# Decode kernel, last stage: output projection by heads from 1 KB rows, head sums normalised straight into the tile of the queries, batches 0 to 6 at low priority

## The chip, the cores and the metric

One core of one Trainium2 chip. The metric is the device time of one execution in microseconds (us). Each result below is a median of several executions, and a ratio to the kernel before from executions on the same chip in alternation. The profile is one execution. Executions of one and the same kernel spread by some 6 us here (1141.9 to 1148.5 for the kernel before in one series), so a microsecond is read from a trace, stage by stage, and the total only confirms it.

In the profiles PE is TensorE and PEld its weight loads, DVE is VectorE, ACT ScalarE, POOL GpSimd, and SP SyncE, which issues the transfers. A pair is one weight load and its matmul. "[2.52 <-issue]" means 2.52 us of idle time in which the engine waited for nothing that the profile shows; I call that a stop. The granted clock is given as a share of full speed.

## The reference, cut to what matters

```python
B, Sq, D = 8, 1, 512;  Hq, Hkv, Sk, Dh = 32, 8, 8192, 128;  F = 1792     # bf16
x = x + A(layernorm(x))      # q = x@wq; softmax(q k^T / sqrt(Dh)) v over the caches; @ wo
x = x + B(layernorm(x))      # silu(x@w1) @ w2
x = x + A(layernorm(x))      # the same caches and weights once more
x = x + B(layernorm(x))
```

The two caches are 268 MB. K and V of a (batch, group) pair are 2 MB each. The kernel keeps the turned keys of one batch on the chip and reuses them for the second layer, but V is read once in each layer. A group is one cache head with its four query heads.

## The kernel before: the parts concerned

Every piece of work is a node with an engine, an assumed duration, a priority (a lower number goes first) and its dependences. A planner runs the nodes on a model clock and emits them in that order.

The sums of one unit (batch, group) are evacuated, gathered over partitions on PE, and multiplied with wo. The kernel multiplies a row of the sums with the row of wo that lies on the same partition. It loads wo so that a partition holds four neighbouring rows, 4 KB in one run, and brings the sums into that arrangement by four matmuls ("spread") and a masked product ("own"):

```python
wo_v = A_wo.rearrange("(g p j) d -> p g (j d)", g=G, j=R)          # 4 KB runs
...
hn = plan.add(f"hi{u}", "ACT", 0.42, high, pr - 2, [vs[-1]])       # L1034, after the last V quarter
ln = plan.add(f"lo{u}", "DVE", 0.45, low, pr - 2, [hn, ...])       # L1038
es.append(plan.add(f"g{u}", "PE", 0.2, gather, pr - 2, [ln, ...])) # L1046
if not h["own_rows"]:        # batches 0 to 6, second layer: normalise into qab
    h["n"] = plan.add(f"n{u}", "DVE", 0.17, norm, pr - 2, [es[-1], h["rc"]])
else:                        # first layer, and batch 7: copy, spread, own
    n = plan.add(f"cast{u}", "ACT", 0.2, cast, pr - 2, [es[-1]])
    n = plan.add(f"spread{u}", "PE", 0.2, spread, pr - 2, [n])     # L1068
    h["n"] = plan.add(f"own{u}", "DVE", 0.17, own, pr - 2, [n, h["rc"], ...])
```

The last stage: the V units of batch 7 (groups 2 to 7) go into the slots of the keys as these are scored, the last one in parts of half, quarter, quarter. wo is read whole (2 x 2 MB) just ahead of them. Batches 0 to 6 go through the second layer's projection and FFN together ("d"), batch 7 alone at the end ("e").

```python
load_wo_all()
w = free_yt[0]
done = [h["n"] for h in ends] + [made[1]["n"], second_q[G - 1]]
for g in range(G):
    w = out_proj_b("d", g, fin, w, done)         # prio = count[0] - G: ahead of all V units
w = x2_node("d", 0, fin, count[0] - G, [w])
fed = ffn_nodes("d", count[0] - G, 0, fin, [w, second_q[G - 1]])
for g, h in enumerate(made):
    if g > 1:
        values(h, at=g)                          # V from a key slot
    ...
    w = out_proj_a(h, w, h["u"])
n = x2_node("e", fin, 1, big, [w])
n = ffn_nodes("e", big, fin, 1, [n, fed])
```

## Time and profile before

| | before |
|---|---|
| time, median of 4 executions | 1144.05 us (1143.73 to 1146.1) |
| span of the profiled execution | 1141.4 us |
| DMA queue busy, share of the span | 98.2% |
| PE / DVE busy | 63% / 53% |
| last V byte lands | 1122.6 us |
| last V quarter starts on PE | 1128.4 us |

Only the last stage changes, so the page's shares of the whole span say little. The two last rows are what matters: the stream ends at 1122.6 us and the work behind it takes 18.8 us more. The prediction below shows the lines for both.

### The profile page before, as it was taken

The numbers are of one execution on the slowest core, as the hardware profiler recorded it, in microseconds if no ns is written. First come the engines' busy times: TensorE is split into PE (matmuls) and PEld (weight loads), VectorE is DVE, ScalarE is ACT, GpSimd is POOL, SyncE is SP. The second block draws the span as 40 slices with busy tenths as digits, with TensorE's granted clock in tenths as the row PEclk, the third lists the DMA queues.
The fourth block names the chain that finished last, engine by engine and source line by source line (L and its number), as shares of the span: only waits on it lengthen the run. The fifth ranks groups of instructions, "written<-read, shape, count | busy, mean of one in ns | idle before, by whom it ended". The sixth has DMA issues, their size and how long they took to land.

```text
span 1141.4 us, 32325 instructions
## 1 busy us (share of the span) xinstructions
PE 717.8 (63%) x13900; PEld 397.8 (35%) x13900; DVE 609.9 (53%) x1768; ACT 155.1 (14%) x517; POOL 117.4 (10%) x295
## 2 busy tenths in 40 slices
PE   2545566676665765656665766567656576565886
PEld 1322333343332433324332433334333243333554
DVE  5753566626664356634666355752656535663341
ACT  0010111111111111111111121111211111111111
POOL 1000011000110001100111000100111000110110
PEclk9665686657776666766666575755767666775675
DMA  9999999999999999999999999999999999999992
GB/s 370 420 418 399 375 412 422 412 390 413 422 421 402 409 418 420 419 393 395 414 421 420 382 419 417 423 400 389 420 424 418 405 409 419 421 422 398 387 424 113
DMA packets 75855, 458.78 MB, mean 402 GB/s; under 512 B 8112, under 2 KB 9920, under 8 KB 48064
## 3 DMA queue, kind: packets, MB, share of 16 engines
q1 hardware_dynamic: 75712, 456.70, 98.2%
q8 instruction: 110, 1.80, 0.6%
q14 instruction: 33, 0.27, 0.1%
HBM read 456.66 MB, written 0.01 MB: 400 GB/s over the span
## 4 chain that ended last, share of the span: by engine, by line
DMA 66%; PE 20%; DVE 6%; issue 5%; ACT 1%; SPq 1%; POOL 1%; POOLq 0%; DVEq 0%; ACTq 0%
DMA ring<-in_A_v_cache_dram 49%; DMA ring<-in_A_wo_dram 8%; PE sc L898 8%; PE ot L1024 7%; DMA kts<-in_A_k_cache_dram 4%; DVE kts L843 3%; DMA kts<-in_A_v_cache_dram 2%; DMA w<-in_B_w_dram 2%; PE misc L725 1%; DMA ring<-in_A_wq_dram 1%; SPq L414 1%; PE ex L1046 1%; PE yt L1098 1%; PE sc L930 1%; DVE part L1038 1%
## 5 line engine op out<-in xcount | busy, mean ns | idle before, releaser
L1024 PE MATMUL ot<-ring,p 128*8 128x256 bf16 x3904 | 240.0, 371 | 185.3 <-DMA ring<-in_A_v_cache_dram 176.3
L843 DVE STREAM_TRANSPOSE kts<-kts 128x1024 uint32<-128x1024 uint32 x256 | 308.1, 1223 | 28.1 <-DMA kts<-in_A_k_cache_dram 27.9
L898 PE MATMUL sc<-kts,bd 128*32 128x256 bf16 x4096 | 284.2, 407 | 33.7 <-DVE kts L843 18.7
L1024 PEld LDWEIGHTS ot<-ring,p 128*8 128x8 bf16 x3904 | 86.0, 96 | 259.9 <-DMA ring<-in_A_v_cache_dram 220.2
L898 PEld LDWEIGHTS sc<-kts,bd 128*32 128x32 bf16 x4096 | 117.5, 117 | 106.3 <-DVE bd L881 26.6
L924 ACT ACTIVATE p<-sc,small 128x256 bf16<-128x256 f32 x128 | 60.8, 475 | 410.0 <-DVE small L919 266.5
L915 POOL PARTITION_ALL_REDUCE small<-small x128 | 47.8, 373 | 616.8 <-DVE small L911 529.0
L1038 DVE TENSOR_TENSOR part<-ot,p 128x256 bf16<-128x256 f32 x128 | 53.1, 415 | 97.6 <-ACT p L1034 56.6
L1034 ACT ACTIVATE p<-ot 128x256 bf16<-128x256 f32 x128 | 49.1, 384 | 410.0 <-PE ot L1024 402.2
L930 PE MATMUL sc<-p,ident 128*32 128x256 bf16 x512 | 42.8, 322 | 82.4 <-ACT p L924 81.4
L881 DVE TENSOR_TENSOR bd<-sc,mask 128x64 bf16<-128x64 f32 x128 | 27.7, 216 | 104.3 <-PE sc L898 98.9
L944 POOL PARTITION_ALL_REDUCE small<-small x128 | 55.4, 433 | 227.5 <-DVE small L940 227.5
L910 DVE TENSOR_REDUCE small<-sc 128x1 f32<-128x256 f32 x128 | 53.3, 416 | 34.6 <-PE sc L898 34.6
L937 DVE STREAM_TRANSPOSE p<-sc 128x256 bf16<-128x256 bf16 x128 | 56.7, 443 | 9.3 <-PE sc L930 6.8
L930 PEld LDWEIGHTS sc<-p,ident 128*32 128x32 bf16 x512 | 15.2, 108 | 110.7 <-ACT p L924 109.0
L1098 PE MATMUL yt<-z,ring 128*128 128x4 bf16 x1024 | 36.8, 166 | 20.5 <-DMA ring<-in_A_wo_dram 19.9
L1046 PE MATMUL ex<-diag,p 128*128 128x4 bf16 x256 | 25.9, 171 | 33.8 <-DVE part L1038 19.0
L1098 PEld LDWEIGHTS yt<-z,ring 128*128 128x128 bf16 x1024 | 31.4, 102 | 43.1 <-DMA ring<-in_A_wo_dram 30.2
L1046 PEld LDWEIGHTS ex<-diag,p 128*128 128x128 bf16 x256 | 16.5, 104 | 77.6 <-ACT p L1034 44.5
L940 DVE TENSOR_SCALAR small<-hm,small 128x4 f32<-128x4 f32 x128 | 27.0, 211 | 29.6 <-ACT p L924 29.2
L1075 DVE TENSOR_TENSOR z<-ex,rc 128x16 bf16<-128x16 f32 x72 | 12.0, 166 | 55.1 <-PE ex L1068 54.8
L919 DVE SCALAR_TENSOR_TENSOR small<-small,hm 128x4 f32<-128x4 f32 x128 | 19.3, 151 | 39.7 <-POOL small L915 39.7
(102 smaller groups left out, 549.7 us busy)
## 6 DMA issues: line engine op xcount, KB each, us to landing
ring<-in_A_v_cache_dram SPq DMA_DIRECT2D x146, 1024.0 KB, 12.5
kts<-in_A_k_cache_dram SPq DMA_DIRECT2D x64, 2048.0 KB, 12.1
ring<-in_A_v_cache_dram SPq DMA_DIRECT2D x196, 512.0 KB, 7.7
ring<-in_A_wo_dram SPq DMA_DIRECT2D x64, 512.0 KB, 12.0
ring<-in_A_wq_dram SPq DMA_DIRECT2D x20, 512.0 KB, 12.4
kts<-in_A_v_cache_dram SPq DMA_DIRECT2D x5, 2048.0 KB, 23.9
kts<-in_A_wo_dram SPq DMA_DIRECT2D x2, 2048.0 KB, 14.2
w<-in_B_w_dram SPq DMA_DIRECT2D x2, 1792.0 KB, 14.9
```

The lines of the kernel that those rows point to most:

```text
L843: op(dve, lambda: dve.transpose(v, v), reads=[], writes=[res("kt", g)], add=(q > 0))
L898: steps.append(lambda t=t, y=y, w=w: pe.matmul(sc[32 * t:32 * t + 32, 0:256], w, kv[:, 2 * t + y, q], start=(q == 0 and y == 0), stop=(q = ...
L910: op(dve, lambda: dve.tensor_reduce(mxr[si], sv, AX.X, ALU.max), reads=[res(*scr)], writes=[res("mxr", si)])
L924: op(act, lambda: act.activation(pt[:, :], sv, ACT.Exp, bias=bias[si], scale=SM_SCALE, accum_out=rsum[si]), reads=[res(*scr), res("bias", ...
L930: steps = [lambda P=P: pe.matmul(sc[32 * P:32 * P + 32, 256:512], src[:, P], pt[:, :], start=True, stop=True) for P in range(4)]
L937: op(dve, lambda: dve.transpose(pt[:, :], src), reads=[res(*scr)], writes=[res("p", sm)])
L944: op(pool, lambda: pool.partition_all_reduce(ssa[si], ssm[si], 128, bass.bass_isa.ReduceOp.add), reads=[res("mxp", si)], writes=[res("mxa" ...
L1024: steps.append(lambda t=t, c=c, k=k: pe.matmul(ot[32 * t:32 * t + 2 * R, 0:2 * DH], pt[:, k:k + 2 * R], vt[:, c, t], start=(P == 0 and c = ...
L1034: op(act, lambda: act.activation(pt[:, :], ot[:, 0:2 * DH], ACT.Copy), reads=[res("ot", o)], writes=[res("p", sm)])
L1038: op(dve, lambda: dve.tensor_tensor(part[:, :], ot[:, 0:2 * DH], pt[:, :], ALU.subtract), reads=[res("ot", o), res("p", sm)], writes=[res( ...
L1046: steps.append(lambda k=k, src=src, y=y: pe.matmul(EX[:, 0:R], src[:, y * DH:y * DH + DH], diag[:, R * y:R * y + R], start=(k == 0 and y = ...
L1098: steps.append(lambda j=j, dt=dt: pe.matmul(YT[:, dt * R:(dt + 1) * R], w[:, j, dt * 128:(dt + 1) * 128], zt[:, R * j:R * j + R], start=(g ...
```

## The change

The intent is less PE work in the last stage and a punctual PE. wo is read so that a partition holds one row of each head (1 KB runs). Then the normalised sums are multiplied with it as they are: no copy, spread or mask. The first residual needs no sum over j. Batches 0 to 6 come last in the choice of what PE does next.

```diff
-        own_rows = layer == 0 or b == NB - 1
+        own_rows = layer == 0
...
-    def out_proj_b(tag, g, nb, prev, deps):     # spread (PE), own (DVE), mul (PE) per group
-        prio = count[0] - G
-        ...
+    def out_proj_b(tag, g, b0, nb, prio, deps): # mul only, straight from qab
+            w = slot(WO_AT[g // 4]).rearrange("p (h d) -> p h d", h=16)
+                        YT[:, dt * nb:(dt + 1) * nb], w[:, R * (g % 4) + r, dt * 128:(dt + 1) * 128],
+                        qab[:, b0:b0 + nb, R * g + r], ...
...
+    def x2_of(tag, b0, nb, prio, deps):         # one add in place of reduce and add
...
-                dma(sp, slot(k).rearrange("p (g n) -> p g n", g=4), wo_v[:, 4 * i:4 * i + 4, :], ksem[k],
+                dma(sp, slot(k).rearrange("p (h d) -> p h d", h=16),
+                    A_wo.rearrange("(h p) d -> p h d", p=128)[:, 16 * i:16 * i + 16, :], ksem[k],
...
+    mid = count[0] + 20
     for g in range(G):
-        w = out_proj_b("d", g, fin, w, done)
+        w = out_proj_b("d", g, 0, fin, mid, [w] + done)
-    w = x2_node("d", 0, fin, count[0] - G, [w])
-    fed = ffn_nodes("d", count[0] - G, 0, fin, [w, second_q[G - 1]])
+    w = x2_of("d", 0, fin, mid, [w])
+    fed = ffn_nodes("d", mid, 0, fin, [w, second_q[G - 1]])
     for g, h in enumerate(made):
         if g > 1:
             values(h, at=g)
-        ...
-        w = out_proj_a(h, w, h["u"])
+        w = out_proj_b("e", g, fin, 1, h["u"], [h["n"], w])
```

Two assumed durations of the planner (variance and root for seven batches) were raised as well; they only place nodes.

More of the change, by code (lines that the diff above doesn't have):

```diff
@@ L490, in _build @@
     big_hs = tail[:, 512:512 + FT * NB]
-    big_y = tail[:, 768:768 + 2 * NB * KT].bitcast(FP32)
     def norm_nodes(tag, prio, b0, nb, deps):
@@ L558, in norm_nodes @@
         a = plan.add(f"{tag}.squares", "PE", 0.05 + 0.2 * nb, squares, prio, [a, x])
-        v = plan.add(f"{tag}.var", "DVE", 0.3, vari, prio, [a])
-        r = plan.add(f"{tag}.root", "POOL", 0.65, root, prio, [v])
+        v = plan.add(f"{tag}.var", "DVE", 0.3 if nb == 1 else 0.6, vari, prio, [a])
+        r = plan.add(f"{tag}.root", "POOL", 0.65 if nb == 1 else 1.6, root, prio, [v])
         return plan.add(f"{tag}.xn", "DVE", 0.3, apply, prio, [r])
@@ L1105, in out_proj_a @@
         return n
-    def out_proj_b(tag, g, nb, prev, deps):
-        prio = count[0] - G
-        hd = slice(R * g, R * g + R)
-        n_c = nb * R
-        zb = tail[:, 1024 + R * n_c * (g % 2):1024 + R * n_c * (g % 2 + 1)]
-        def spread():
-            steps = [lambda j=j: pe.matmul(
-                EX[:, 32 + n_c * j:32 + n_c * (j + 1)], rows_of(j), qab[:, 0:nb, hd], start=True, stop=True)
-                for j in range(R)]
-            mms(steps, reads=[res("ident")] + [res("attnb", g, b) for b in range(nb)], writes=[res("ex")])
-        def own():
-            op(dve, lambda: dve.tensor_tensor(
-                zb.rearrange("p (n h) -> p n h", h=R),
-                EX[:, 32:32 + R * n_c].rearrange("p (n h) -> p n h", h=R),
-                mask[:, :].unsqueeze(1).to_broadcast([128, R * nb, R]), ALU.mult),
-                reads=[res("mask")], writes=[res("ex"), res("ring", 1)])
+    def out_proj_b(tag, g, b0, nb, prio, deps):
@@ L1127, in mul @@
         def mul():
-            w = slot(WO_AT[g // 4]).rearrange("p (g j d) -> p g j d", g=4, j=R)[:, g % 4]
+            w = slot(WO_AT[g // 4]).rearrange("p (h d) -> p h d", h=16)
             steps = []
-            for j in range(R):
+            for r in range(R):
                 for dt in range(KT):
-                    steps.append(lambda j=j, dt=dt: pe.matmul(
-                        YT[:, dt * n_c:(dt + 1) * n_c], w[:, j, dt * 128:(dt + 1) * 128],
-                        zb[:, n_c * j:n_c * (j + 1)],
-                        start=(g == 0 and j == 0 and dt == 0), stop=(g == G - 1 and j == R - 1),
+                    steps.append(lambda r=r, dt=dt: pe.matmul(
+                        YT[:, dt * nb:(dt + 1) * nb], w[:, R * (g % 4) + r, dt * 128:(dt + 1) * 128],
+                        qab[:, b0:b0 + nb, R * g + r],
+                        start=(g == 0 and r == 0 and dt == 0), stop=(g == G - 1 and r == R - 1),
@@ L1136, in mul @@
                         skip_group_check=True))
-            mms(steps, reads=[res("wo_all", g // 4), res("ring", 1)], writes=[res("yt")], add=g > 0)
-        n = plan.add(f"{tag}.sp{g}", "PE", 0.2, spread, prio, deps + zb_own[-1:])
-        zb_own.append(plan.add(f"{tag}.own{g}", "DVE", 0.25, own, prio, [n] + zb_mul[-2:-1]))
-        zb_mul.append(plan.add(f"{tag}.w{g}", "PE", 0.56, mul, prio, [zb_own[-1], wo_all[g // 4], prev]))
-        return zb_mul[-1]
-    zb_own = []
-    zb_mul = []
+            mms(steps, reads=[res("wo_all", g // 4)] + [res("attnb", g, b) for b in range(b0, b0 + nb)],
+                writes=[res("yt")], add=g > 0)
@@ L1147, in _build @@
+        return plan.add(f"{tag}.w{g}", "PE", 0.54, mul, prio, deps + [wo_all[g // 4]])
     free_yt = [None]
@@ L1177, in load_ffn, with x2_node, add @@
             sp, w2_sb[:, :, :], B_w2.rearrange("(ft p) d -> p ft d", p=128), wsem["w2"], writes=[res("w2")]), ring=False))
-    def x2_node(tag, b0, nb, prio, deps):
-        ys = ysum[:, :] if nb == 1 else big_y[:, 0:KT * nb]
+    def x2_node(b, prio):
         def add():
             op(dve, lambda: dve.tensor_reduce(
-                ys, YT[:, 0:KT * nb * R].rearrange("p (k h) -> p k h", h=R), AX.X, ALU.add),
-                reads=[res("yt")], writes=[res("ysum")] + ([] if nb == 1 else [res("ring", 1)]))
+                ysum[:, :], YT[:, 0:KT * R].rearrange("p (k h) -> p k h", h=R), AX.X, ALU.add),
+                reads=[res("yt")], writes=[res("ysum")])
+            op(dve, lambda: dve.tensor_tensor(xs[:, b, :], ysum[:, :], xs[:, b, :], ALU.add),
+               reads=[res("ysum"), res("xs")], writes=[res("xs")])
+        return plan.add(f"c{b}.x2", "DVE", 0.3, add, prio, [y_now[0]])
+    def x2_of(tag, b0, nb, prio, deps):
+        def add():
             op(dve, lambda: dve.tensor_tensor(
-                xs[:, b0:b0 + nb, :], ys.rearrange("p (k b) -> p b k", b=nb), xs[:, b0:b0 + nb, :], ALU.add),
-               reads=[res("ysum"), res("xs")], writes=[res("xs")])
-        return plan.add(f"{tag}.x2", "DVE", 0.3, add, prio, deps)
+                xs[:, b0:b0 + nb, :], YT[:, 0:KT * nb].rearrange("p (k b) -> p b k", b=nb), xs[:, b0:b0 + nb, :],
+                ALU.add), reads=[res("yt"), res("xs")], writes=[res("xs")])
+        return plan.add(f"{tag}.x2", "DVE", 0.2, add, prio, deps)
     WO_AT = (0, 1)
@@ L1226, in _build @@
         if b >= 0:
-            n = x2_node(f"c{b}", b, 1, prio, [y_now[0]])
+            n = x2_node(b, prio)
             free_yt[0] = n
@@ L1285, in _build @@
             values(h, at=g)
-        h["wo"] = wo_all[g // 4]
-        h["wo_in"] = lambda g=g: (
-            slot(WO_AT[g // 4])[:, GR * (g % 4):GR * (g % 4 + 1)], [res("wo_all", g // 4)])
-        w = out_proj_a(h, w, h["u"])
+        w = out_proj_b("e", g, fin, 1, h["u"], [h["n"], w])
     big = count[0] + 10
-    n = x2_node("e", fin, 1, big, [w])
+    n = x2_of("e", fin, 1, big, [w])
     n = ffn_nodes("e", big, fin, 1, [n, fed])
```

## The prediction

> **What bounds the kernel now.** I read the page first: the slices and the DMA queue.
>
> ```profile
> DMA  9999999999999999999999999999999999999992
> GB/s 370 420 418 399 375 412 422 412 390 413 422 421 402 409 418 420 419 393 395 414 421 420 382 419 417 423 400 389 420 424 418 405 409 419 421 422 398 387 424 113
> q1 hardware_dynamic: 75712, 456.70, 98.2%
> ```
>
> The queue is full in 39 of 40 slices and empty in most of the last one. The kernel is a stream of 456.7 MB and then a tail with no transfer in it. The change touches only what follows the last keys, so its worth is in two terms: when the last byte lands, and how long the work behind it takes. I therefore took busy times by stretch for the end.
>
> ```profile
> core 0: us, PE busy (x) PEld busy (x) DVE busy (x) ACT busy (x) POOL busy (x), PEclk, DMA share, GB/s
> 1092.00:1098.00 6.00, 4.51 (x112) 3.13 (x108) 3.84 (x20) 1.13 (x4) 1.24 (x3) 1.00 1.01 428
> 1098.00:1122.00 24.00, 19.03 (x477) 13.34 (x477) 4.13 (x18) 2.37 (x9) 1.54 (x1) 0.52 0.94 393
> 1122.00:1128.40 6.40, 5.42 (x100) 2.88 (x97) 1.20 (x4) 0.90 (x4) 0.00 (x0) 0.50 0.01 3
> 1128.40:1132.20 3.80, 1.75 (x36) 1.02 (x33) 0.94 (x4) 0.56 (x2) 0.00 (x0) 0.50 0.00 0
> 1132.20:1141.40 9.20, 4.46 (x130) 3.92 (x130) 1.59 (x5) 0.39 (x2) 0.55 (x1) 0.50 0.02 4
> ```
>
> Read the DMA share downwards: the stream is over near 1122, yet PE is still 85% busy (5.42 of 6.40 us) until 1128.4. That stretch is a backlog. The last quarter of V was issued at about 1095.24 and took 27.4 us, the longest landing in the group of the slot loads, so it landed at about 1122.65. It was multiplied only at 1128.42, 5.8 us later. From there the order of time is a plain chain:
>
> ```profile
> 1128.42 0.60 PE L1024 MATMUL ot<-kts,p 128*8 128x256 bf16 x8
> 1129.07 0.38 ACT L1034 ACTIVATE p<-ot 128x256 bf16<-128x256 f32 x1 [1.99 <-PE ot L1024]
> 1129.55 0.42 DVE L1038 TENSOR_TENSOR part<-ot,p 128x256 bf16<-128x256 f32 x1 [1.70 <-ACT p L1034]
> 1130.17 0.19 PE L1046 MATMUL ex<-diag,part 128*128 128x4 bf16 x2
> 1131.19 0.59 PE L1098 MATMUL yt<-z,kts 128*128 128x4 bf16 x16 [0.27 <-DVE z L1075]
> ```
>
> It ends at 1141.4, 12.98 us after it starts. So the present end is 1122.65 (last landing) + 5.77 (backlog) + 12.98 (chain). The view of the chain of waits shows 25.51 us of "issue" on POOL before 1133.18; that is only POOL with nothing to do since the other batches' root, and I do not read it as a bound.
>
> Why is there a backlog? Batches 0 to 6 of the second layer have the priority of the first unit of this stage. Their norm and both FFN matrices sit between the V units on an engine that runs in order, and the PE loads of this stretch show two stops that nothing else explains:
>
> ```profile
> 1108.82 1.55 PEld L575 LDWEIGHTS misc<-xn,w 128*128 128x128 bf16 x55 [0.75 <-issue]
> 1114.97 1.38 PEld L1024 LDWEIGHTS ot<-kts,p 128*8 128x8 bf16 x32 [2.07 <-issue]
> 1122.62 0.08 PEld L1024 LDWEIGHTS ot<-kts,p 128*8 128x8 bf16 x1 [0.98 <-issue]
> ```
>
> Counting weight loads, 127 pairs lie between the first and second stop and 127 between the second and third. That is 254 instructions, and the waits make it about 256. PE runs 27,800 instructions and the "instruction" queue shows 110 packets in 1.80 MB, that is 16 KB each and about 253 PE instructions per packet. So these look like fetches of PE's own program that came late: 6.2 us from 1108.82 to 1114.97 and 7.65 to the next.
>
> [...] under a full queue three blocks cost 0.75, 2.07 and 0.98 us here. [...] B_w2 has exactly the new layout (rows of 512 bf16, 1 KB), and its stretch beside that of the present wo:
>
> ```profile
> DMA packets 680, 0.70 MB, mean 348 GB/s; under 512 B 0, under 2 KB 680, under 8 KB 680
> ...
> DMA packets 402, 1.68 MB, mean 420 GB/s; under 512 B 7, under 2 KB 7, under 8 KB 393
> ```
>
> The first is 110 to 112 us, 1 KB packets only; the second 1086 to 1090, 4 KB packets. 1 KB is 17% slower. [...] in the trace a weight load of the output projection takes 96 ns with 28 moving columns and 104 with 4, and 16 pairs take 0.47 to 0.51 us either way. So fewer moving columns buy nothing.
>
> **The change part by part.**
>
> 1. *Head spreads out.* For batches 0 to 6, 8 groups x 4 matmuls vanish (line 1115: 32, 2.34 us busy) with 8 DVE masks of 0.272 us (2.2 us). For batch 7, 8 x 4 matmuls (line 1068: 32, 2.36 us), 8 ACT copies of 0.174 us and a DVE op per unit's reciprocal (0.16 us) vanish; the masked product becomes a plain normalisation of about the same 0.17 us. The 128 + 128 projection matmuls stay; their moving operand goes from 28 to 7 and from 4 to 1 columns, which is worth nothing. PE saves about 4.7 us of busy time, half a page of program (64 pairs, 128 instructions), nearly all of it before the last landing.
>
> 2. *On the end chain.* Gather ends 1130.36; copy, spread and product bring z at 1131.13. Afterwards the normalisation reads PSUM at once and ends at about 1130.57: -0.56 us. The first residual is a reduce and an add, 1131.82 to 1132.19; afterwards one add of about 0.2: -0.17, rounded to -0.2 with its gap. Copy, FFN and store are the same instructions: 9.2 us. The chain is 12.98 - 0.56 - 0.2 = 12.2; I take 12.3.
>
> 3. *Low priority.* The batches 0 to 6 come last in the choice of what PE runs next, so PE does them where V has not landed. Does it fit? From 1092 to the start of the last quarter PE was busy 4.51 + 19.03 + 5.42 = 29.0 us, less 2.3 and about 1.8 for the spreads of the units before the last: 24.9 us of work. The time from 1092 to the last landing is 30.7 us, 32.6 with the delay of item 4. So there are 6 to 8 us of slack, of which fetch stops took 3.8 before. The backlog can nearly go. But program supply sets a pace: from the last block boundary before V (pair 648 of my count, about 1095.5) about four more blocks lie before the last quarter, at 6.2 to 7 us each when PE runs fast: 1120 to 1123.5, and then some 45 pairs, about 2 us. This is close to the landing itself, so I leave 0.6 us of backlog in place of 5.77.
>
> 4. *wo in runs of 1 KB.* Two loads of 2 MB, 4.19 MB together: at 420 GB/s 10.0 us, at 350 12.0 us. The queue is full from here to the last byte (shares near 1.0) and the six V units come behind it, so the end of the stream moves by +2.0 us: last landing 1124.65. Its own lateness does not matter: the second half of wo is first needed in the gaps before 1099.
>
> Sum: 1124.65 + 0.6 + 12.3 = 1137.55 against 1141.4, -3.85 us. Applied to the median: 1143.78 - 3.85 = 1139.9 us, 0.34% faster.
>
> **The rivals.**
>
> *The backlog stays.* The order is fixed from assumed durations: 0.4 us for a quarter of V where half-clock PE takes about 0.5 per quarter, and it knows no fetch stop. If the norm, up and down of the seven batches land in front of the last V units, PE is late as before. For it: the granted clock of 0.50 and the fetch pace, which the cut of half a page eases little. Against it: 6 to 8 us of slack and V units 5 us apart with under 3 us of PE work each. Then only the saved PE work counts, with the stream's delay hidden in the backlog: -1 to -3 us, 1141 to 1143.
>
> *The 1 KB runs cost nothing more here*[...]. Then the landing stays at 1122.65, the fetch pace becomes the bound, and I would see -5 to -5.9 us: 1138 to 1139. Against it: 348 GB/s over pure 1 KB packets in this very trace.
>
> *The stream's delay takes the whole gain.* For this wo would have to cost some 5 us or more, under 290 GB/s. A wait for the late wo at the head of PE's order would do the same. I see nothing for it but the untested larger count of packets beside fetches; the time would be 1142 to 1145.
>
> [...] the granted clock is 0.99 to 1.00 between 1078 and 1098 and 0.50 after. If the new order kept it high, all PE pieces would be shorter[...]. [...]
>
> **Range and chances.** The main sum gives 1139.9. The rival with free 1 KB runs is the low side, the kept backlog the high side; I give the main line some 55%, the kept or half-kept backlog 25%, free runs 15%, the rest 5%. The range for 8 in 10 is 1137.6 to 1143.0. The whole tail after the stream is 18.7 us, 1.6% of the time, so 2% faster is out of reach, and a loss of 23 us would need a new stall that nothing here hints at: 0.01, 0.98, 0.01.
>
> **What would show it.** Right: 1024 packets of 4 KB become 4096 of 1 KB, so packets under 2 KB rise by about 4096; the stretch of wo shows about 350 GB/s; the last V lands about 2 us later; PE idles in 1098 to 1122 on V transfers, which it hardly does now (0.6 us), and the last quarter starts within 1 us of its landing; from there to the end 12.2 to 12.5 us; the spread rows and the reduce of the first residual are gone in this stage. Wrong: a last quarter that starts 3 us or more after landing (backlog kept), with "issue" gaps 127 pairs apart (program supply) or with the FFN of the seven batches just ahead of it (order); or a stream that ends at 1122.6 (free runs); or a clock near 1.0 after 1122.

## The result, and the profile after

| | before | after |
|---|---|---|
| time, median of 4 | 1144.05 us | 1142.51 us (1142.25 to 1144.96) |
| ratio | | 0.9988, 95% interval 0.9969 to 1.0006 |

A ratio is the mean time of one kernel's fast executions over that of the other's in the same rounds, so it is not quite the ratio of the medians. The time lies within the predicted range, 2.6 us above the predicted 1139.9. In a second series the unaltered change gave 0.9986 (0.9962 to 1.001).

The profiled execution of the changed kernel is the longest of its four (1144.96 us). It is already 4.7 us behind the trace of before when the last stage begins, although PE's program is the same up to its last 100 or so grouped rows. So I count the stage from its first V issue (1078.16 us before, 1082.85 after). The table gives every run that was traced in this way; "late" is the start of the last V quarter less its landing (issue plus time to landing).

| run | first V lands | last V lands | last quarter starts | late | from there to the end | end |
|---|---|---|---|---|---|---|
| before | 19.80 | 44.40 | 50.26 | 5.86 | 12.96 | 63.23 |
| after | 20.91 | 45.79 | 48.15 | 2.37 | 12.23 | 60.38 |
| after, again | 21.35 | 46.57 | 48.50 | 1.93 | 12.23 | 60.73 |
| before_1k | 21.08 | 45.58 | 52.06 | 6.48 | 12.96 | 65.02 |
| after_4k | 19.00 | 44.76 | 46.95 | 2.19 | 12.23 | 59.17 |
| before_low | 23.54 | 48.04 | 50.22 | 2.19 | 12.96 | 63.18 |
| after_high | 22.45 | 46.97 | 52.71 | 5.75 | 12.28 | 64.99 |
| before_pad64 | 21.29 | 46.16 | 50.67 | 4.52 | 12.97 | 63.65 |
| after_pad64 | 22.52 | 47.04 | 47.14 | 0.10 | 12.22 | 59.36 |
| pad64_again | 21.39 | 46.40 | 46.76 | 0.35 | 12.23 | 58.98 |
| after_pad96 | 21.92 | 47.15 | 47.40 | 0.26 | 12.21 | 59.62 |
| after_pipe | 21.00 | 46.92 | 47.17 | 0.25 | 12.18 | 59.34 |
| pipe_pad64 | 22.32 | 47.25 | 47.36 | 0.11 | 12.16 | 59.52 |
| burst (its end holds 384 more pairs) | 21.38 | 45.91 | 48.20 | 2.29 | 22.03 | 70.23 |

The zero point is an issue that waits for PE's scoring, and the queue ahead of it is not equally long in all runs, so the columns counted from zero carry about 1 us of scatter (more in before_low and before_pad64, where wo was issued 6.3 and 7.3 us before the zero point and not about 8.5). "Late" and "from there to the end" don't depend on it.

So the stage is 2.85 us shorter in one trace and 2.5 in the other: landing +1.4 to +2.2, lateness -3.5 to -3.9, final chain -0.73. The same stretches of the changed kernel, with the columns as in the prediction:

```profile
1102.70:1126.70 24.00, 16.80 (x406) 11.52 (x407) 3.47 (x15) 1.78 (x5) 1.53 (x1) 0.51 0.99 414
1126.70:1131.10 4.40, 3.73 (x80) 2.16 (x76) 0.59 (x2) 0.38 (x1) 0.00 (x0) 0.50 0.13 51
1131.10:1134.00 2.90, 1.38 (x32) 0.74 (x24) 0.72 (x3) 0.38 (x1) 0.00 (x0) 0.50 0.00 0
1134.00:1143.20 9.20, 4.46 (x130) 3.92 (x130) 1.62 (x6) 0.39 (x2) 0.55 (x1) 0.50 0.01 3
```

PE is busy 16.8 of 24 us beside the stream where it was 19.0, and 3.7 of 4.4 us in the next stretch, where it was 5.4 of 6.4. That stretch begins 1.9 us before the last landing (1128.64) here; behind the landing PE is still busy for 1.7 us, where it was 5.3. PE has less to do, is idle for longer, and is late nevertheless. Its weight loads show three stops again:

```profile
1106.52 0.10 PEld L1023 LDWEIGHTS ot<-kts,p 128*8 128x8 bf16 x5 [1.55 <-issue]
...
1112.60 1.01 PEld L574 LDWEIGHTS misc<-xn,w 128*128 128x128 bf16 x35 [0.81 <-issue]
...
1119.11 0.72 PEld L1023 LDWEIGHTS ot<-kts,p 128*8 128x8 bf16 x16 [2.52 <-issue]
```

They follow each other by 6.1 and 6.5 us. Counting back from the end of the program, they stand at 587, 458 and 329; counted in this way those of before stood at 522, 394 and 265. This count, which all expectations below use, takes the weight loads (the page counts 13836 of them and 13836 matmuls, so these are nearly pairs) together with 6 to 10 semaphore and drain instructions that the trace puts among them; the weight loads alone give 577, 449 and 322. With matmuls, weight loads and these others, exactly 256 instructions of PE lie between one stop and the next (255 and 256 in before).

The trace also holds the cause itself. The packets of its instruction queue q8 have 16 KB (109 of them for PE's 27981 instructions, 110 for 28109 in before, so about one in 256), and one landed at 1105.16, 1111.17 and 1117.80: PE went on 1.36, 1.43 and 1.31 us later. (The stops of before ended 1.36 to 1.47 us after such a landing, and those at the boundaries in the other runs below 1.28 to 1.55 us.) After a stop the next packet began 3.55 and 4.10 us later and took 1.1 us, which adds up to the 6.1 and 6.5 us (5.88 us later after the third stop; 3.72 and 5.14 after the first two of before). When the stream was over, in before, it began 1.30 us after the last stop.

The third stop lies in the middle of group 4, the third of the six V units that come from slots. After it PE never waits for a transfer again, and still loses time in each unit:

```profile
1122.44 1.88 PE L1023 MATMUL ot<-kts,p 128*8 128x256 bf16 x32
1125.41 0.19 PE L1045 MATMUL ex<-diag,p 128*128 128x4 bf16 x2 [1.09 <-DVE part L1037]
1125.46 0.19 PE L1045 MATMUL ex<-diag,part 128*128 128x4 bf16 x2
1125.91 0.59 PE L1114 MATMUL yt<-qab,kts 128*128 128x1 bf16 x16 [0.26 <-DVE qab L1055]
1126.43 2.31 PE L1023 MATMUL ot<-kts,p 128*8 128x256 bf16 x40
```

A unit is multiplied (32 matmuls), then PE waits 1.09 us for ACT and DVE to evacuate it, gathers, waits again, projects, and only then starts the next unit, whose V landed at 40.8, that is at 1123.7, almost 3 us ahead of 1126.43. The fixed order holds PE at the gather. In the kernel before, quarters of the next unit and the old "own" chain lay in such gaps. The waits of the gather for DVE in this stage, before and after (us in total, times, longest):

```profile
PE ex L1046 <- DVE part L1038: 1.3, 2, 1.1
```

```profile
PE ex L1045 <- DVE part L1037: 3.9, 4, 1.1
```

wo is slower as predicted. A stretch of pure 1 KB packets in the changed kernel, and the packets of its whole page:

```profile
DMA packets 677, 0.70 MB, mean 349 GB/s; under 512 B 2, under 2 KB 676, under 8 KB 676
```

```profile
DMA packets 78926, 458.76 MB, mean 401 GB/s; under 512 B 8112, under 2 KB 14016, under 8 KB 51136
```

Packets under 2 KB were 9920 before; the difference is the 4096 of wo. They also hold up the issue of the next load, the first V unit, by 10 us (10.37 in before_1k, 0.33 in after_4k; 10.1 to 11.7 us in the ten traces with wo in 4096 packets, 0.3 to 2.9 in the four with 1024); before and after:

```profile
1078.16 0.33 SPq L414 DMA_DIRECT2D kts<-in_A_v_cache_dram  x1
```

```profile
1082.85 10.09 SPq L414 DMA_DIRECT2D kts<-in_A_v_cache_dram  x1
```

That costs nothing here: the load is needed 20 us later, and the queue is full of work ahead of it.

### The profile page after: what moved, and what is told of

The parts are those of the page before. It is cut to its first block, busy times and chain, and to the rows that moved or that the text cites. A ratio compares the mean times of both kernels' runs of the same rounds, so it can differ in the third digit from the quotient of the medians.

```text
span 1143.2 us, 32166 instructions
## 1 busy us (share of the span) xinstructions
PE 715.6 (63%) x13836; PEld 395.4 (35%) x13836; DVE 605.6 (53%) x1750; ACT 153.5 (13%) x509; POOL 116.9 (10%) x295
## 4 chain that ended last, share of the span: by engine, by line
DMA 67%; PE 19%; DVE 6%; issue 5%; ACT 2%; SPq 1%; POOL 1%; POOLq 0%; DVEq 0%; ACTq 0%
DMA ring<-in_A_v_cache_dram 53%; DMA ring<-in_A_wo_dram 9%; PE sc L897 8%; PE ot L1023 7%; DVE kts L842 3%; DMA kts<-in_A_k_cache_dram 2%; DMA kts<-in_A_v_cache_dram 2%; DMA w<-in_B_w_dram 2%; PE misc L724 1%; PE yt L1097 1%; PE ex L1045 1%; ACT ring L755 1%; SPq L414 1%; PE sc L929 1%; DVE part L1037 1%
## 5 line engine op out<-in xcount | busy, mean ns | idle before, releaser
L1023 PE MATMUL ot<-ring,p 128*8 128x256 bf16 x3904 | 243.2, 375 | 186.2 <-DMA ring<-in_A_v_cache_dram 178.1
## 6 DMA issues: line engine op xcount, KB each, us to landing
ring<-in_A_wo_dram SPq DMA_DIRECT2D x64, 512.0 KB, 11.7
kts<-in_A_v_cache_dram SPq DMA_DIRECT2D x5, 2048.0 KB, 20.9
```

Of the source, the lines that this page charges most:

```text
L1023: steps.append(lambda t=t, c=c, k=k: pe.matmul(ot[32 * t:32 * t + 2 * R, 0:2 * DH], pt[:, k:k + 2 * R], vt[:, c, t], start=(P == 0 and c = ...
```

## The experiments

Theory A after the first look: in the last stage PE is late because its own program arrives at one block of 256 instructions per 6.1 to 6.6 us while the DMA queue is full, and because the order lets each unit wait out its evacuation. Theory B: the 1 KB runs take the gain on the path. In the expectations, "fourth V unit" means group 4 in the changed kernel and group 3 in the kernel before. A further question was which part of the change made PE less late. The wrong layouts of wo give a wrong projection on purpose. The comparison with the reference did not object, so its tolerance doesn't see this term and its verdict says nothing about these two runs. Nor does it vouch for the projection of the changed kernel: that its rows of wo meet the right heads rests on reading the code.

### wo in 4 KB runs in the changed kernel (after_4k)

```diff
-                dma(sp, slot(k).rearrange("p (h d) -> p h d", h=16), A_wo.rearrange("(h p) d -> p h d", p=128)[...], ...
+                dma(sp, slot(k).rearrange("p (g n) -> p g n", g=4), wo_v[:, 4 * i:4 * i + 4, :], ksem[k], ...
```

> The changed kernel with wo in runs of 4 KB again (its output is wrong on purpose, the rows of wo lie elsewhere). All times are counted from the issue of the first V load of the last stage. In the changed kernel the last V quarter lands at 45.8, starts 2.4 us later at 48.15 and the end is at 60.4. Theory A (PE is late because its own program comes late, one block of 256 instructions per 6.1 to 6.6 us under a full queue, and because each V unit waits out its own evacuation): landing falls by 1.4 us to 44.4, the start stays within 0.5 us of 48.15, end 60.0 to 60.6. Theory B (the 1 KB runs take the gain on the path): landing falls by 1.4 us and start and end fall with it, end near 59.0.

Median 1139.78 us, ratio to before 0.9967 (0.9947 to 0.9987). The last V lands 1.0 us earlier than in the first trace of the change, and the last quarter and the end come 1.2 us earlier (59.17); against the second trace it is 1.8, 1.6 and 1.6. Lateness stays at 2.19. That is what B expected of this run, and A's "start stays" is refuted: PE's lateness is no store of slack. This does not rest on the zero point: had the start stayed while the landing fell by 1.4 us, lateness would have grown to 3.8. The table shows why. The whole PE part starts when the first V unit lands (20.9 against 19.0), and what is lost after that is lost from there.

### wo in 1 KB runs in the kernel before (before_1k)

```diff
-                dma(sp, slot(k).rearrange("p (g n) -> p g n", g=4), wo_v[:, 4 * i:4 * i + 4, :], ksem[k], ...
+                dma(sp, slot(k).rearrange("p (h d) -> p h d", h=16), A_wo.rearrange("(h p) d -> p h d", p=128)[...], ...
```

> The kernel before with wo in runs of 1 KB (output wrong on purpose). Before: landing at 44.4, last quarter at 50.26, end at 63.23 from the first V issue of the stage. Theory A: landing moves to 45.8, last quarter and end stay within 0.5 us, the delay is hidden in the backlog of 5.9 us. Theory B: end moves by the same 1.4 us to 64.6.

Median 1146.1 us, ratio 1.0012 (0.9992 to 1.0032). Landing +1.2, end +1.8 (65.02), with PE 6.5 us late. Again B; had the backlog hidden the delay, lateness would have fallen to about 4.5. PE's own waits in this stage, of before and of this run, show where the delay enters:

```profile
PE ot L1024 <- DMA kts<-in_A_v_cache_dram: 0.6, 1, 0.6
```

```profile
PE ot L1024 <- DMA kts<-in_A_v_cache_dram: 1.8, 1, 1.8
```

The columns are us in total, times, longest. There is one wait in each, at the first V unit, and it is 1.2 us longer: just the delay of the landing. Everything behind it moves along. A backlog of 6 us that forms after this wait hides nothing that comes before it.

### 64 pairs of small matmuls at the very start (after_pad64)

```diff
+    def pad():
+        mms([lambda: pe.matmul(EX[:, 0:4], ident[:, :], ident[:, 0:4], start=True, stop=True)] * 64,
+            reads=[res("ident")], writes=[res("ex")])
+    plan.add("pad", "PE", 0.0, pad, -20, [c_n])
```

> The changed kernel with 64 small matmul pairs at the very start, while PE has nothing to do. They move each block boundary of PE's program by 64 pairs towards the start of the stage and change nothing else. Theory A (the stops marked as issue are late fetches of program blocks): the stops now stand 587, 458 and 329 plus 64 pairs (651, 522, 393) and 265 from the end instead of 587, 458 and 329; as the boundary no longer falls into the fourth V unit, the last quarter starts 0.5 to 1.5 us after landing instead of 2.4, end 59.0 to 59.9. Rival (the stops belong to certain waits of the program): they stay at 587, 458 and 329 pairs, 0.8 to 2.5 us each, end 60.4.

Median 1138.27 us, ratio 0.9951 (0.9933 to 0.9969): adding instructions made the kernel faster. In the last stage the stops stand at 650 and 393, and none at 587, 458 or 329. At 522 and 265, where boundaries were expected too, no stop shows; PE came to these 1.7 us or more after the landing of the block:

```profile
1097.98 0.19 PEld L1120 LDWEIGHTS yt<-qab,kts 128*128 128x128 bf16 x4 [1.82 <-issue]
...
1110.65 1.36 PEld L592 LDWEIGHTS misc<-ring,w 128*128 128x128 bf16 x48 [0.59 <-issue]
```

The first one now falls into the time before the first V unit has landed, where it costs nothing, and the one of 2.52 us is gone. Lateness is 0.10 us, below the expected 0.5 to 1.5. So these stops belong to a place in PE's instruction stream and not to what the instructions do. The waits for V that the prediction had looked for appear here: its weight loads wait 3.0 us in total, in four places, for V in the slots, where those of the change waited 0.5.

### The gather behind the next unit's first half (after_pipe)

```diff
         if g > 1:
             values(h, at=g)
+        if g > 2:
+            made[g - 1]["g_n"].deps.append(h["vs"][1])     # gather of g-1 after two quarters of g
```

> The changed kernel with one more dependence: the gather of a V unit comes after the first two quarters of the next unit, so that its evacuation lies beside them. Theory A with the order as its second half: from the fourth unit on PE saves about 1 us a unit, the last quarter starts within 1.2 us of its landing, end 59.0 to 59.4. If the program supply alone makes PE late, the stops grow by what the order saves, and the end stays within 0.4 us of 60.4.

Median 1139.54 us, ratio 0.9964 (0.9945 to 0.9982). Lateness 0.25, end 59.34, as A expected. One stop of 1.17 us remains in the V part, at 586; the ones at 458 and 329 don't show although the boundaries are still there. The weight loads wait 6.0 us for V in the slots in place of 0.5, and PE passes these boundaries 2.2 and 1.3 us after the landing of the block. A missing stop is not the gain, though: PE passes the boundary at 329 36.0 us after the zero point, the changed kernel 36.3. Behind it the weight loads wait 3.5 us for V in this run, in the changed kernel for none, so it is the order that lets the units catch up. Either mend alone is enough: if the stop comes elsewhere, or if the units can catch up afterwards, PE is punctual.

### The changed kernel at the old priority (after_high)

```diff
-    mid = count[0] + 20
+    mid = count[0] - G
```

> The changed kernel with its priority undone: batches 0 to 6 at the old, high priority, heads and 1 KB runs as in the change. Counted from the first V issue of the stage, lateness is the start of the last quarter less its landing: 5.9 us before, 2.4 after. If the low priority made PE punctual, lateness goes back to 5 us or more and the end to 63. If the removed head spreads did it (64 pairs, half a program block, and 4.7 us of PE time), lateness stays at 1.5 to 3.5 us and the end at 59.5 to 61.5.

Median 1146.8 us, ratio 1.0017 (0.9992 to 1.0043); lateness 5.75, end 64.99. This fits "the priority made PE punctual", but a second thing is mixed in. At the high priority the root of the seven batches comes before the last keys' reduction on POOL, and that reduction came late:

```profile
1105.16 1.52 POOL L539 TENSOR_TENSOR rstd<-var,expo 128x7 f32<-128x7 f32 x1 [8.70 <-DVE ring L550]
1115.00 0.39 POOL L914 PARTITION_ALL_REDUCE small<-small  x1 [8.31 <-issue]
```

Between the two the trace has two MODIFY_POOL_CONFIG instructions, at 1106.91 and 1106.95, which the timeline leaves out. Two such instructions also stand between a root and the next reduction in the traces of before and after, and there that reduction started 5.9 to 9.5 us after the root had ended (the first root of the program aside); some of these waited for DVE as well, and how much of the time belongs to these instructions was not tested. DVE waited 5.29 us for the reduction, and PE 4.44 us for DVE. In the kernel before the root came after the last reduction, so this stop is not in the backlog of before. The run does not single out the priority.

### The kernel before at the low priority (before_low)

```diff
-        prio = count[0] - G           # out_proj_b; the same for x2_node and ffn_nodes of "d"
+        prio = count[0] + 20
```

> The kernel before with only the priority of the change (4 KB runs, spreads kept). If the low priority made PE punctual: lateness 2 to 3.5 us in place of 5.9, landing unchanged at 44.4, end 60 to 61. If the spreads did: lateness 5 us or more, end 62.5 to 64.

Median 1141.48 us, ratio 0.9972 (0.9951 to 0.9993). Lateness 2.19 in place of 5.86, with all spreads kept. So the priority is enough to get the whole gain of lateness that the change shows. Its boundaries stand at the same counts from the end, but other work lies around them, and there is no stop over 0.45 us from the unit of group 4 on, where before had 0.98 and, just ahead of that unit, 2.07. I can't tell how much of the 3.7 us is order and how much is where the boundaries came to lie. The expected landing (44.4) and end (60 to 61) did not come: landings read 3.6 to 3.7 us later and the end, 63.18, looks unmoved. Of this, 2.2 us are the zero point, which lies that much nearer to the issue of wo; the other 1.4 us are not explained. Counted from the issue of wo the end comes 2.2 us earlier than in before (69.5 against 71.7).

### PE's program by itself (burst)

The changed kernel with 384 pairs of the same small matmuls twice: after batch 3's second norm, in the middle of the stream, and after batch 7's last projection, with nothing in the queue.

> The supply of PE's program by itself: the changed kernel with 384 pairs of small matmuls twice, once in the middle of the stream (queue full) and once after the last V unit (queue empty). If a block of 256 instructions comes late only because its fetch stands behind the stream: in the first burst PE stops every 127 to 128 pairs, blocks follow at 6.1 to 6.6 us; in the second there is no stop over 0.5 us, blocks follow at the pace of the matmuls, some 4 us. If the fetch takes that long by itself, both bursts stop alike. The total grows by about 12 us or more for the second burst.

1162.81 us, one execution. The first two lines are the burst in the stream, the last one that behind it:

```profile
519.13 3.28 PEld L1202 LDWEIGHTS ex<-ident 128*128 128x128 bf16 x120
524.66 6.95 PEld L1202 LDWEIGHTS ex<-ident 128*128 128x128 bf16 x256 [2.25 <-issue]
...
1141.62 10.32 PEld L1202 LDWEIGHTS ex<-ident 128*128 128x128 bf16 x384
```

384 pairs take 10.3 us behind the stream, 27 ns each or 3.4 us a block, without a stop. In the stream there is one stop of 2.25 us, then none of note. The expected series did not come, and the reason is in the experiment: the burst held up what frees the V cells, so the stream itself ran dry:

```profile
516.00:524.00 8.00, 5.48 (x161) 4.07 (x160) 0.91 (x3) 0.38 (x1) 0.55 (x1) 0.50 1.00 395
524.00:530.00 6.00, 5.34 (x199) 5.34 (x199) 0.00 (x0) 0.00 (x0) 0.00 (x0) 0.50 0.16 61
```

The DMA share fell from 1.00 to 0.16, and with it the stops went. The stop ended 1.28 us after a packet of PE's program had landed, and the next packet began 1.13 us after it, not 3.6 to 4.1 as in the last stage. So in these traces a block is late only beside a full queue. The pace of 6.1 to 6.5 us under load rests on the traces of the stage, not on this run.

### Both mends together (pipe_pad64)

> Both mends together (64 pairs at the start, gather behind the next unit's first half). Each alone brought lateness to 0.1 and 0.25 us, so both together can bring no more if the landing now bounds the end: lateness 0 to 0.6 us, 12.2 us from there to the end, time within 1.5 us of the better of the two (1138.3). If something else still held PE back, another 1 us or more would come off.

Median 1140.21 us, ratio 0.9953 (0.993 to 0.9975); lateness 0.11, end 59.52. No better than either mend alone: the landing bounds the end now. (The median is 1.9 us above 1138.3 and not within 1.5 as expected, but that figure is from another series; the ratios to before agree, 0.9953 and 0.9951.)

### The changed kernel and the pad on one chip again (after_again, pad64_again)

> The changed kernel once more, unaltered, to narrow its ratio to before, which was 0.9988 with an interval of about 0.0018 to either side. From the parts counted after the first V issue of the stage (landing +1.1 to 1.4, lateness -3.5, last chain -0.7) it should be 2 to 3 us faster, ratio 0.9975 to 0.9983; a ratio of 0.999 or more would say that something ahead of the last stage gives 1 us back.

Median 1144.24 us, ratio 0.9986 (0.9962 to 1.001). Between the two expectations; the interval holds both. Its trace repeats the first one: stops 587, 458 and 329 from the end, of 1.45, 0.75 and 2.51 us.

> The changed kernel with 64 pairs at the start once more, beside the changed kernel on the same chip. Program supply: lateness 0 to 0.5 us where the changed kernel has 2 to 2.6, and 1.5 to 4 us faster than it in the median. If the first result was the luck of that chip, less than 1 us.

Median 1138.0 us, ratio 0.9937 (0.9914 to 0.9961); the mean of its six executions is 5.6 us under the mean of the changed kernel's six, more than the 1.5 to 4 us expected. Lateness 0.35 against 1.93. The last stage explains 1.8 of the 5.6 us (58.98 against 60.73). The other 3.8 us must come from ahead of it; the two profiled executions even differ by 7.7 us there (their zero points are at 1074.26 and 1081.98). The stream's own scatter and stops of the same kind in the earlier stages are both candidates; I have not separated them.

### 96 pairs (after_pad96)

> The changed kernel with 96 pairs at the start. Program supply: boundaries at 683, 554, 426 and 297 pairs from the end, stops of 0.5 to 1.3 us at some of these and none elsewhere, lateness between those of 64 pairs (0.1) and none (2.4): 0.3 to 1.6 us. If any change of the start helps and not the place of the boundary, lateness stays at 0.1.

Median 1138.74 us, ratio 0.9942 (0.9917 to 0.9966). Stops 682, 554 and 426 pairs from the end, of 0.99, 0.91 and 0.65 us, within a pair of the places named. Lateness is 0.26, a little under the expected 0.3 to 1.6, since all three stops lie ahead of the V unit of group 4. The places of the stops confirm the block; the lateness doesn't rank the two pads.

### 64 pairs before the kernel before (before_pad64)

> The kernel before with 64 pairs at the start. Its boundaries move to 586 to 589, 458 and 329 from the end; the stop of 2.07 us within the last quarter of the fourth unit goes, one of about 1 us comes within the first FFN matrix. Program supply as a part of its backlog: lateness 3.5 to 4.8 us instead of 5.9, end 1 to 2.3 us earlier. If the order alone made the backlog, lateness stays at 5.4 to 6.4.

Median 1141.83 us, ratio 0.9973 (0.995 to 0.9996). Stops at 458 (1.14 us) and 329 (0.81 us); those of 2.07 and 0.98 us are gone. Lateness 4.52 in place of 5.86, as expected of program supply. The expected earlier end did not come: 63.65 is 0.4 us later, as this run's landings read up to 1.8 us later; counted from the issue of wo it is 0.8 us earlier (70.9 against 71.7). So some 1.3 us of the old backlog were a matter of where the boundaries lay; the rest would be order and work, which this run doesn't separate. This is one trace against one, and the same boundaries gave 5.86 in before and 6.48 in before_1k.

## Why the prediction was right or wrong

The time lay in the range and within 2%. The predicted gain of 3.85 us came out as 2.5 to 2.9 us in the stage, and as 1.4 and 1.6 us in the total (0.12% and 0.14% of 1144), with intervals of 2 to 3 us either way. The total is therefore no proof of the main line: 1142.5 lies where the prediction put its kept backlog (1141 to 1143), while the stage shows three fifths or more of the backlog gone. That the total fell into the range owes something to what happened ahead of the stage.

1. *wo in 1 KB runs, +2.0 us.* Right. 349 GB/s against 418 over pure 4 KB packets of after_4k, which is 12.0 against 10.0 us for 4.19 MB. The landing moved by 1.4 and 2.2 us in the two traces of the change and by 1.2 in before_1k. B_w2's row of the same trace was the right witness.
2. *The chain from the last quarter, 12.3 us.* Right: 12.23 twice, against 12.96. Fewer moving columns were indeed worth nothing: 16 pairs of the projection took 0.51 us with one column as with four. (Nor did a weight load's own columns count for much: behind 1098 us in before, loads of 8 columns took 98 ns in the mean and loads of 128 took 105.)
3. *The backlog, 0.6 us in place of 5.77.* This term was mis-sized. It measured 2.37 and 1.93 us, and that is the 1.3 to 1.8 us that the stage lacks. The step took the slack as one sum (24.9 us of work in 32.6 us, stops of 3.8) and the program's pace as one end time ("1120 to 1123.5, and then some 45 pairs"). Both treat time as if it could be regained. A stop of 2.52 us fell into the V unit of group 4, and from there the order, V, gather, projection, next V, left 1.09 us of evacuation open in each unit, so PE caught up only slowly. The prediction counted four blocks at 6.2 to 7 us each. In the changed kernel three took 6.1 to 6.5 us, but the fourth took 10.3 (1119.11 to 1129.37), although its successor had landed 3.3 us before it was needed: there the order set the pace and not the supply. after_pad64 and after_pad96 move the stop and lateness falls to 0.10 and 0.26; after_pipe fills the gap and it falls to 0.25.
4. *PE saves 4.7 us and half a block.* The 64 pairs went (13900 to 13836). But before_low shows the same lateness without that saving, so PE's punctuality doesn't need the work removed; what the removal gave for certain is the 0.73 us of the final chain.
5. *The rival "the backlog stays ... with the stream's delay hidden in the backlog".* The stops 127 to 129 pairs apart came as named there, and a third to two fifths of the backlog stayed. The second half was wrong in its logic: before_1k and after_4k show that a later or earlier stream moves the end by about as much even when PE is 2 to 6 us late, as PE waits for the first V unit and the backlog forms behind that wait.
6. *What the profile would show.* PE waiting on V transfers and a start within 1 us of landing: not in the change (0.5 us of waits), but in after_pad64 (3.0 us). The counts of packets and the missing rows came as written. The clock stayed at 0.50 to 0.51, as the main line had it. What sets it is not shown: in before, PE was busy for 75% of 1092 to 1098 at a clock of 1.00 and for 79% of the next 24 us at 0.52. What a high clock would have been worth differs by piece: in before, eight V matmuls took 0.39 us at 1086.39 and 0.60 at 1128.42, 16 pairs of the other batches' projection 0.56 at 1092.84 and 0.61 at 1101.12.

Open: the 1 us between the gain in the stage and the gain in the total, which is inside the scatter; the 3.8 us that the pads gain ahead of the last stage; and how much of the priority's gain is order rather than the luck of boundaries. The version that was measured twice and beats both kernels is the change with 64 pairs in front, 0.9951 and 0.9937 of before in two series.

## What to carry to other kernels

When an in-order engine is late, ask where in its chain a delay enters: here the slack of a stretch hid nothing that came before the first wait (in before_1k the end moved by 1.8 us with PE 6.5 us late), and little was regained while each unit waited out its own evacuation (1.09 us). If stops without a cause stand a fixed number of instructions apart (256 here), shift the program by half that number (64 pairs here) at a place where it costs nothing: if they move with it, and a packet of the instruction queue lands just before each ends (1.28 to 1.55 us here), it is the program's supply, and where the boundaries fall is a parameter to tune (lateness 2.37 and 1.93 us without the pad, 0.10 and 0.35 with it). Price a new layout by the packets of a transfer of the same run length in the same trace: B_w2 showed 348 GB/s before, and wo then moved at 349.
